# Signs of 64-bit weights as one byte written by GpSimd, two VectorE operations in place of three, each weight tile begun one tile ahead

## The chip, the cores and the metric

One core of a Trainium2 chip runs the kernel. The metric is the device time of one execution in microseconds (us); lower is better. PE is TensorE (its weight loads are PEld), DVE is VectorE, ACT is ScalarE, POOL is GpSimd, SP is SyncE, whose queue issues the transfers.

## The reference

Attention over 8 batches with 8 heads of width 64, on 512 local and 32 global positions, and then a feed-forward layer over the resulting 8 x 544 = 4352 tokens (the kernel works them as eight blocks of 512 local rows and a last one of the 256 global rows):

```python
k_all, v_all = concat(k_g, k_l), concat(v_g, v_l)
out_g = softmax(scale * q_g @ k_all.T) @ v_all              # 32 global rows see all
s_ll = where(|i - j| <= 32, scale * q_l @ k_l.T, -1e9)      # 512 local rows: a band ...
a_l = softmax(concat(scale * q_l @ k_g.T, s_ll))            # ... and the 32 global keys
x = concat(out_g, a_l @ v_all), heads side by side          # tokens x 512
h = x @ w_in                                                # 512 x 2048
g = max(h, 0) + log1p(exp(-abs(h)))
return g @ w_out                                            # 2048 x 512
```

The attention's inputs are 32-bit floats. The two weight matrices arrive as 64-bit floats. The kernel loads them as pairs of 32-bit words and makes 32-bit floats of them on the chip.

## The kernel before

**Stages.** Heads are worked in pairs; m numbers the 32 pairs, four to a batch. The first four pairs (batch 0's, m = 0 to 3, in two parts each) go through a stage written out by hand: scores, `soft0` (the maximum L169, its scaling L170, the exps L172 on ACT, the sums' L178 and L179), diagonal matrices on POOL (L185), `turn0`, `evict0` (L213), `values0` and `split0` (L231). The global rows of that stage use L254 and L255. Every later m goes in pieces with two parts, (m, 0) and (m, 1): scores into the PSUM tiles `s_ps`, copied to SBUF by ACT (L310) or DVE (L312); the maxima by a transposing reduction (L313) and a gather of small operations (POOL L325, DVE L328 to L338); `probs` spreads them as a mask `mb` (two DVE transposes, L346), POOL subtracts it (L355, L357) and ACT takes the exps (L358); the sums by a second transposing reduction (L368) with its own gather (L325 to L332, L371, L375), spread as `rb` (L377); the values into the PSUM tile `v_ps`, scaled by DVE into `xa` (L396). `s_ps` and `v_ps` use banks in turn, so PE can't write the next scores or values into a bank before L310, L312 or L396 has read it. The attention's result is split into a high and a low part, `xh` (L442) and `xl` (L443), whose matmuls together keep the precision.

**Feed-forward.** Its work comes in items between the pieces of attention: an item multiplies `xh` and `xl` by a tile of w_in into `h`; ACT and DVE make softplus of it (L530 to L532 on ACT, `e` by DVE L533), which is split into `gh` (ACT L536) and `gl` (POOL L537), and these are multiplied by tiles of w_out into `o`. The number in `e_5` counts these steps.

**Weights.** There are 32 tiles, 16 of each matrix (`wi`, `wo`), of 128 x 512 pairs of words. One is loaded as `wiraw` or `woraw` and goes through `split_w`:

- `abs_w`: ACT (L470) scales the high word, read as a 32-bit float, by a power of two into `wbits`. That puts its exponent right for the shift that follows.
- `bits_w`: DVE shifts `wbits` left by 3 (L477), puts the sign of the high word in (L479), and puts in the three top bits of the low word (L482). The result stands in the low words' places, or for the last tile of a matrix in `wlast`.
- `halves_w`: ACT rounds it to the matmul's format (L487), and POOL subtracts that from it (L488), which gives the low half.

`wbits` of some tiles, `wlast` and the masks `mb` take turns in two buffers called "mb".

**What sets the order.** PE's order is the order in which the program is written. The other engines' order comes from a scheduler at build time, which follows dependences and priorities, with some pins: `keep` and, in the hand-written stage (while `tight` is true), `note` chain operations of an engine one behind the other; `after(i, "maxima")` holds a weight operation behind the latest maxima on DVE. In the hand-written stage one weight tile is worked per step, for W_PRE = 9 steps; later `weights(upto)` works tiles up to a mark that runs ahead of the items.

Of the kernel before, what the change touches and what calls it, by code (L numbers as in the profile page):

```python
# [19 lines left out]
P = 128  # L20
# [10 lines left out]
NF = DFF // P  # L31
# [32 lines left out]
def moe_over_global_local_attention(  # L64
# [34 lines left out]
    for o, w, base, sign in ((32, 32, 0, 1), (64, 32, -96, -1), (96, 128, 32, 1), (96, 128, 32, -1)):  # L99
        r = mask0[:, 0, 1, o:o + w]  # L100
# [55 lines left out]
    def keep(what, i):  # L156
        order[what] = after(i, what).ins
# [184 lines left out]
    def probs(m, p):  # L342
        s, e = st["s", m, p], st["e", m]
        k = QW[p] // 32
        mb = pl.tile([P, 2, 352], F32, tag="mb", name=f"mb{m}_{p}", bufs=2)
        nc.vector.transpose(mb[:, :, :QW[p]].rearrange("p h (s k) -> p h s k", k=32),  # L346
                            windows(e, FIRST[p], 21, 2, k).unsqueeze(3).to_broadcast([P, 2, k, 32]))

        def pairs(t, width, start, step, w):
            base = t[:, 0, start:start + 1]  # L350
            return bass.AP(base.tensor, base.offset, [list(base.ap[0]), [width, 2], [step, 2], [1, w]])

        for so, sd, mo, md, w in (((0, 352, 0, 192, 160),), ((32, 192, 0, 128, 192),))[p]:
            sw = pairs(s, 512, so, sd, w)
            nc.gpsimd.tensor_tensor(sw, sw, pairs(mb, 352, mo, md, w), op=ALU.subtract)  # L355
        for so, mo, w in (((160, 64, 192),), ((0, 64, 32), (416, 224, 96)))[p]:
            nc.gpsimd.tensor_tensor(s[:, :, so:so + w], s[:, :, so:so + w], mb[:, :, mo:mo + w], op=ALU.subtract)  # L357
        nc.scalar.activation(s, s, AF.Exp, scale=0.125)  # L358
# [87 lines left out]
    wi, wo, raws = {}, {}, {}  # L446
# [13 lines left out]
    def note(what, i):  # L460
        if tight:
            keep(what, i)
        return i

    def abs_w(kind, k):
        if A_LO <= k < NF - A_UP:
            a = pl.tile([P, 512], I32, tag=f"{kind}{k + A_UP}", name=f"wbits{kind}{k}", bufs=1)
        else:
            a = pl.tile([P, 512], I32, tag="mb", name=f"wbits{kind}{k}", bufs=2)
        note("act", nc.scalar.mul(a.bitcast(F32), raws[kind, k][:, :, 1].bitcast(F32), DOWN))  # L470
        return a

    def bits_w(kind, k, a):
        t = raws.pop((kind, k))
        lo32, hi32 = t[:, :, 0], t[:, :, 1]

        i = nc.vector.tensor_scalar(a, a, 3, None, op0=ALU.logical_shift_left)  # L477
        note("dve", i) if tight else after(i, "maxima")
        note("dve", nc.vector.scalar_tensor_tensor(a, hi32, -0x80000000, a, op0=ALU.bitwise_and, op1=ALU.bitwise_or))  # L479

        r = lo32 if k < NF - 1 else pl.tile([P, 512], I32, tag="mb", name=f"wlast{kind}", bufs=2)
        note("dve", nc.vector.scalar_tensor_tensor(r, lo32, 29, a, op0=ALU.logical_shift_right, op1=ALU.bitwise_or))  # L482
        return r.bitcast(F32)

    def halves_w(kind, k, r):
        (wi if kind == "wi" else wo)[k] = o = pl.tile([P, 2, 512], F32R, tag=f"{kind}{k}", name=f"{kind}{k}", bufs=1)
        note("act", nc.scalar.copy(o[:, 0], r))  # L487
        nc.gpsimd.tensor_tensor(o[:, 1], r, o[:, 0].bitcast(F32), op=ALU.subtract)  # L488

    def split_w(kind, k):  # L490
        halves_w(kind, k, bits_w(kind, k, abs_w(kind, k)))

    def output_banks():
        if "o" not in banks:
# [147 lines left out]
    tight, held = True, None  # L642
    for k in range(-2, n - 2):
        stage(k + 2, 0)
        if k == 0:
            key_masks()
        if held:
            r = bits_w(*held)
        stage(k + 2, 1)
        stage(k - 2, 5)  # L650
        stage(k - 2, 6)
        stage(k, 3)
        stage(k, 4)
# [16 lines left out]
    tight = False  # L670
# [74 lines left out]
```

## Time and profile before

| | |
|---|---|
| median of 3 runs | 990.09 us (990.07 to 990.39) |
| the profiled execution's own time | 991.48 us |
| its span in the trace | 989.7 us |
| mean granted TensorE clock | 0.988 |
| busy: PE, PEld | 946.2 us (96%), 763.8 us (77%) |
| busy: DVE, ACT, POOL | 643.1 us (65%), 492.6 us (50%), 469.5 us (47%) |
| the 32 weight tiles on DVE: L477, L479, L482 | 21.5 us, 28.7 us, 29.8 us |
| the 32 weight tiles on POOL: L488 | 45.2 us |

In a row of the timeline stand the start and the duration in us, engine, line, operation, output and inputs; behind it in brackets the idle time of that engine just before and what ended it. In a row that groups operations stand their count, their busy time in us and the mean of one in ns, and behind the second bar the idle time before them. In a row by stretch stand the stretch, its length, the busy time of each engine, the granted clock, the share of the DMA engines and their GB/s. The release of a wait is inferred from the semaphores.

### The profile page before, as it was taken

To read this page: it belongs to the slowest core of one execution; us is meant where nothing else is said; L and a number is where in the kernel's file an instruction comes from. 1 tells how busy PE (TensorE), PEld (TensorE's weight loads), DVE (VectorE), ACT (ScalarE), POOL (GpSimd) and SP (SyncE) were. 2 spreads that over 40 slices of the span, in tenths; PEclk is the share of its full clock that TensorE was granted. 3 is DMA by queue.
4 is the path that set the end of the run, shared out by engine and by line. 5 is a ranking of instruction groups with operands and counts; after the bars stand their busy time and mean duration, and the time that the engine had idled before them with its cause. 6 is when DMAs were issued, how large, how long until landed. Compare 5 with 4: busy or idle time off the path is not lost.

```text
span 989.7 us, 14732 instructions
## 1 busy us (share of the span) xinstructions
PE 946.2 (96%) x5476; PEld 763.8 (77%) x5476; DVE 643.1 (65%) x1193; ACT 492.6 (50%) x811; POOL 469.5 (47%) x648
## 2 busy tenths in 40 slices
PE   6998598889999999999999999999999999999998
PEld 4776476668888788878887888878887888888896
DVE  5869898896667756786669666776668665411211
ACT  5756466544444544454445444454454445444453
POOL 4437776655445544444445544554445444322221
PEclk8998899999999999999999999999999999999999
DMA  9651331211112211121112111121112100100000
GB/s 357 231 188 46 122 111 57 65 66 41 47 47 69 69 47 46 48 74 47 47 37 72 47 47 47 66 71 47 47 33 88 32 17 1 65 1 1 10 35 22
DMA packets 30697, 64.60 MB, mean 65 GB/s; under 512 B 7328, under 2 KB 7840, under 8 KB 30624
## 3 DMA queue, kind: packets, MB, share of 16 engines
q1 hardware_dynamic: 29888, 63.32, 19.0%
q8 instruction: 43, 0.70, 0.3%
q10 hardware_dynamic: 736, 0.33, 0.2%
q14 instruction: 30, 0.25, 0.1%
HBM read 54.20 MB, written 9.44 MB: 64 GB/s over the span
## 4 chain that ended last, share of the span: by engine, by line
PE 67%; DVE 9%; POOL 4%; issue 3%; ACT 1%; DMA 1%; POOLq 0%; DVEq 0%; ACTq 0%
PE o L132 30%; PE h L132 29%; PE s_ps L132 5%; PE v_ps L132 4%; DVE xh L442 1%; DVE zt L368 1%; DVE xl L443 1%; POOL xl L443 1%; DVE mb L346 1%; POOL mt L325 1%; DVE s L312 1%; POOL s L355 1%; DVE xa L396 1%; DVE mt L332 0%; DVE e L533 0%
## 5 line engine op out<-in xcount | busy, mean ns | idle before, releaser
L132 PE MATMUL h<-xh,wi 128*128 128x512 f32 (+1 forms) x1152 | 341.9, 380 | 6.5 <-DVE e L533 5.8
L132 PE MATMUL o<-wo,gh 128*128 128x512 f32 x1088 | 344.8, 398 | 0.0
L537 POOL TENSOR_TENSOR gl<-e,gh 128x512 fp32r<-128x512 f32 x136 | 180.5, 1327 | 315.7 <-ACT gh L536 263.2
L132 PEld LDWEIGHTS h<-xh,wi 128*128 128x128 f32 x1152 | 211.1, 188 | 51.8 <-DVE e L533 8.9
L132 PEld LDWEIGHTS o<-wo,gh 128*128 128x128 f32 x1088 | 198.8, 188 | 46.0 <-issue 3.3
L533 DVE SCALAR_TENSOR_TENSOR e<-h,e 128x512 f32<-128x512 f32 x136 | 92.7, 682 | 210.1 <-ACT e L532 192.5
L132 PE MATMUL h<-xl,wi 128*128 128x512 f32 (+1 forms) x576 | 217.6, 378 | 0.9 <-DVE xl L443 0.9
L132 PE MATMUL o<-wo,gl 128*128 128x512 f32 x544 | 213.1, 392 | 0.2
L530 ACT ACTIVATE e<-h 128x512 f32<-128x512 f32 x136 | 81.0, 595 | 175.5 <-PE h L132 173.5
L536 ACT CAST gh<-e 128x512 fp32r<-128x512 f32 x136 | 84.5, 622 | 154.7 <-DVE e L533 154.5
L132 PEld LDWEIGHTS h<-xl,wi 128*128 128x128 f32 x576 | 108.4, 188 | 21.7 <-DVE xl L443 1.3
L355 POOL TENSOR_TENSOR s<-s,mb 128x640 f32<-128x640 f32 (+1 forms) x56 | 96.6, 1725 | 57.8 <-DVE mb L346 57.8
L132 PEld LDWEIGHTS o<-wo,gl 128*128 128x128 f32 x544 | 102.4, 188 | 23.2 <-POOL gl L537 1.1
L368 DVE TRANSPOSE_TENSOR_REDUCE zt<-s 128x32 f32<-128x1024 f32 x56 | 69.4, 1239 | 58.9 <-ACT s L358 58.7
L358 ACT ACTIVATE s<-s 128x1024 f32<-128x1024 f32 x56 | 59.4, 1061 | 83.5 <-POOL s L357 47.7
L532 ACT ACTIVATE e<-e,one 128x512 f32<-128x512 f32 x136 | 98.4, 723 | 4.3
L531 ACT ACTIVATE e<-e 128x512 f32<-128x512 f32 x136 | 85.9, 632 | 3.9
L313 DVE TRANSPOSE_TENSOR_REDUCE mt<-s 128x32 f32<-128x1024 f32 x56 | 68.9, 1231 | 3.7 <-ACT s L310 2.9
L132 PE MATMUL s_ps<-raw 64*128 64x192 f32 (+2 forms) x672 | 64.3, 325 | 0.6 <-issue 0.6
L132 PEld LDWEIGHTS v_ps<-s,v 128*64 128x64 f32 x896 | 49.4, 137 | 19.5 <-ACT s L310 6.5
L132 PE MATMUL v_ps<-s,v 128*64 128x96 f32 (+3 forms) x896 | 56.7, 280 | 7.3 <-ACT s L310 5.2
L132 PEld LDWEIGHTS s_ps<-raw 64*128 64x128 f32 x672 | 53.5, 192 | 11.6 <-issue 10.8
(147 smaller groups left out, 886.0 us busy)
## 6 DMA issues: line engine op xcount, KB each, us to landing
raw<-in_qk SPq DMA_DIRECT2D x32, 352.0 KB, 3.0
v<-in_v SPq DMA_DIRECT2D x28, 384.0 KB, 3.0
raw<-in_qk SPq DMA_DIRECT2D x28, 368.0 KB, 3.6
wiraw<-in_w_in SPq DMA_DIRECT2D x16, 512.0 KB, 8.5
woraw<-in_w_out SPq DMA_DIRECT2D x16, 512.0 KB, 7.4
out<-ot SPq DMA_DIRECT2D x32, 256.0 KB, 2.1
v<-in_v SPq DMA_DIRECT2D x4, 512.0 KB, 8.6
raw<-in_qk SPq DMA_DIRECT2D x4, 416.0 KB, 8.3
```

Source lines behind the costliest of these rows:

```text
L132: order["pe"] = after(nc.tensor.matmul(*a, **k), "pe").ins
L313: order["scores"] = nc.vector.tensor_reduce(windows(mt, 4 + 16 * p, 36, 2, 16), s.rearrange("p h (b k) -> p h b k", k=32), axis=AX.X, op=A ...
L355: nc.gpsimd.tensor_tensor(sw, sw, pairs(mb, 352, mo, md, w), op=ALU.subtract)
L358: nc.scalar.activation(s, s, AF.Exp, scale=0.125)
L368: nc.vector.tensor_reduce(windows(zt, 4 + 16 * p, 36, 2, 16), st["s", m, p].rearrange("p h (b k) -> p h b k", k=32), axis=AX.X, op=ALU.add ...
L443: (nc.vector if j % 2 else nc.gpsimd).tensor_tensor(lo, f(t), hi.bitcast(F32), op=ALU.subtract)
L530: nc.scalar.activation(e, ph, AF.Abs)
L531: nc.scalar.activation(e, e, AF.Exp, scale=-1.0)
L532: nc.scalar.activation(e, e, AF.Ln, bias=one)
L533: nc.vector.scalar_tensor_tensor(e, ph, 0.0, e, op0=ALU.max, op1=ALU.add)
L536: nc.scalar.copy(gh, e)
L537: nc.gpsimd.tensor_tensor(gl, e, gh.bitcast(F32), op=ALU.subtract)
```

## The change

DVE's three operations on a tile become two, and POOL gets a small one:

- `signs_w` (new): DVE shifts the low word right by 29 in place (new L475), which leaves its three top bits at the bottom and zeros above. POOL (new L477) compares the high word, read as a float, with 0, multiplies by 128, and writes the result as one byte, the top byte of that shifted low word.
- `bits_w`: one DVE operation (new L483) shifts `wbits` left by 3 and puts in the low word with its sign byte.
- `begin_w` (new): a tile's `signs_w` and `abs_w`; `weights` calls it for a tile and for the one behind it ahead of `split_w`. The pin behind the maxima is now on L475, no longer on the shift of `wbits`.
- In the hand-written stage `begin_w` is called where `abs_w` was, at the end of the step before; L475 is chained there, so it stands ahead of the next L169.
- The buffers "mb" are three, no longer two.

The later lines move by the inserted ones: L487 and L488 become L488 and L489, L530 to L533 become L541 to L544, L536 and L537 become L547 and L548.

```diff
-        mb = pl.tile([P, 2, 352], F32, tag="mb", name=f"mb{m}_{p}", bufs=2)
+        mb = pl.tile([P, 2, 352], F32, tag="mb", name=f"mb{m}_{p}", bufs=3)
...
+    def signs_w(kind, k):
+        t = raws[kind, k]
+        note("dve", i := nc.vector.tensor_scalar(t[:, :, 0], t[:, :, 0], 29, None, op0=ALU.logical_shift_right))
+        b = t.rearrange("p c w -> p (c w)").bitcast(mybir.dt.uint8).rearrange("p (c b) -> p c b", b=8)
+        nc.gpsimd.tensor_scalar(b[:, :, 3], t[:, :, 1].bitcast(F32), 0.0, 128.0, op0=ALU.is_lt, op1=ALU.mult)
+        return i
+
     def bits_w(kind, k, a):
         t = raws.pop((kind, k))
-        lo32, hi32 = t[:, :, 0], t[:, :, 1]
-
-        i = nc.vector.tensor_scalar(a, a, 3, None, op0=ALU.logical_shift_left)
-        note("dve", i) if tight else after(i, "maxima")
-        note("dve", nc.vector.scalar_tensor_tensor(a, hi32, -0x80000000, a, op0=ALU.bitwise_and, op1=ALU.bitwise_or))
-
-        r = lo32 if k < NF - 1 else pl.tile([P, 512], I32, tag="mb", name=f"wlast{kind}", bufs=2)
-        note("dve", nc.vector.scalar_tensor_tensor(r, lo32, 29, a, op0=ALU.logical_shift_right, op1=ALU.bitwise_or))
+        r = t[:, :, 0] if k < NF - 1 else pl.tile([P, 512], I32, tag="mb", name=f"wlast{kind}", bufs=3)
+        note("dve", nc.vector.scalar_tensor_tensor(r, a, 3, t[:, :, 0], op0=ALU.logical_shift_left, op1=ALU.bitwise_or))
         return r.bitcast(F32)
...
+    begun = {}
+
+    def begin_w(kind, k):
+        if (kind, k) not in begun:
+            i = signs_w(kind, k)
+            if not tight:
+                after(i, "maxima")
+            begun[kind, k] = abs_w(kind, k)
+        return kind, k, begun[kind, k]
+
     def split_w(kind, k):
-        halves_w(kind, k, bits_w(kind, k, abs_w(kind, k)))
+        halves_w(kind, k, bits_w(*begin_w(kind, k)))
...
             if order_w[wk[1]]:
+                begin_w(*order_w[wk[1]])
+                if wk[1] + 1 < len(order_w) and order_w[wk[1] + 1]:
+                    begin_w(*order_w[wk[1] + 1])
                 split_w(*order_w[wk[1]])
...
         if -1 <= k and wk[1] < W_PRE:
-            held = order_w[wk[1]]
-            held += (abs_w(*held),)
+            held = begin_w(*order_w[wk[1]])
```

PE's order is the same before and after. DVE's order at three places follows. In a row stand the line, the operation, the output and its input, and the shape; a number at the end of a name only tells tiles apart, and the one or two before it say which part (`xa_0` is m = 4's, `xa_1` m = 5's; `e_5` the fifth step).

First, DVE in the hand-written stage, one step near 43 us; before:

```order
L213 COPY p_1_0gl<-t_1_0_348 96x512
L169 TENSOR_REDUCE sums_1_376<-s_2_1_368 128x4
L170 TENSOR_SCALAR sums_1_376<-sums_1_376 128x4
L477 TENSOR_SCALAR wbitswi_366<-wbitswi_366 128x512
L479 SCALAR_TENSOR_TENSOR wbitswi_366<-wiraw_127,wbitswi_366 128x512
L482 SCALAR_TENSOR_TENSOR wiraw_127<-wiraw_127,wbitswi_366 128x512
L178 TENSOR_SCALAR sums_1_376<-sums_1_376 128x4
```

and after:

```order
L213 COPY p_1_0gl<-t_1_0_348 96x512
L475 TENSOR_SCALAR wiraw_127<-wiraw_127 128x512
L169 TENSOR_REDUCE sums_1_378<-s_2_1_370 128x4
L170 TENSOR_SCALAR sums_1_378<-sums_1_378 128x4
L483 SCALAR_TENSOR_TENSOR wiraw_127<-wbitswi_368,wiraw_127 128x512
L178 TENSOR_SCALAR sums_1_378<-sums_1_378 128x4
```

The three operations between L170 and L178 became one, and the new shift stands between L213 and L169.

Second, DVE around L396 of m = 4, which frees the PSUM bank for which PE stands at 120.37 us; before (from e_4 on):

```order
L313 TENSOR_REDUCE mt_906<-s_1_1048 128x2x16
...
L338 COPY mt_906<-mt_906 32x40 x3
L477 TENSOR_SCALAR wbitswo_1121<-wbitswo_1121 128x512
L477 TENSOR_SCALAR wbitswo_1175<-wbitswo_1175 128x512
L477 TENSOR_SCALAR wbitswo_1290<-wbitswo_1290 128x512
L346 STREAM_TRANSPOSE mb_0_1064<-mt_906 128x704
L346 STREAM_TRANSPOSE mb_1_1069<-mt_906 128x2x320
L479 SCALAR_TENSOR_TENSOR wbitswo_1121<-woraw_953,wbitswo_1121 128x512
L533 SCALAR_TENSOR_TENSOR e_5_1110<-h_5_1087,e_5_1110 128x512
L396 TENSOR_TENSOR xa_0_1146<-v_ps_1129,rb_981 128x384
```

and after:

```order
L313 TENSOR_REDUCE mt_910<-s_1_1052 128x2x16
L483 SCALAR_TENSOR_TENSOR wiraw_932<-wbitswi_1035,wiraw_932 128x512
L328 TENSOR_REDUCE zt_967<-zt_967 32x6x2 x2
...
L375 RECIPROCAL zr_980<-zt_967 32x19 x4
L377 STREAM_TRANSPOSE rb_985<-zr_980 128x608
L396 TENSOR_TENSOR xa_0_1150<-v_ps_1133,rb_985 128x384
L396 TENSOR_TENSOR xa_0_1150<-v_ps_1133,rb_985 128x224
L544 SCALAR_TENSOR_TENSOR e_5_1114<-h_5_1091,e_5_1114 128x512
L328 TENSOR_REDUCE mt_910<-mt_910 32x6x2 x2
```

L396 stood behind the gather and the transposes of the next maxima; now it stands ahead of them, behind its own sums' gather, and ahead of e_5.

Third, DVE ahead of L396 of m = 5, for which PE stands at 148.77 us; before:

```order
L533 SCALAR_TENSOR_TENSOR e_8_1371<-h_8_1348,e_8_1371 128x512
L332 COPY mt_1192<-mt_1192 32x6
L338 COPY mt_1192<-mt_1192 32x40 x3
L346 STREAM_TRANSPOSE mb_0_1337<-mt_1192 128x704
L346 STREAM_TRANSPOSE mb_1_1342<-mt_1192 128x2x320
L396 TENSOR_TENSOR xa_1_1419<-v_ps_1402,rb_1248 128x384
```

and after:

```order
L368 TENSOR_REDUCE zt_1234<-s_0_912 128x2x16
L368 TENSOR_REDUCE zt_1234<-s_1_1052 128x2x16
...
L544 SCALAR_TENSOR_TENSOR e_8_1375<-h_8_1352,e_8_1375 128x512
...
L346 STREAM_TRANSPOSE mb_0_1341<-mt_1196 128x704
L346 STREAM_TRANSPOSE mb_1_1346<-mt_1196 128x2x320
L475 TENSOR_SCALAR wiraw_1218<-wiraw_1218 128x512
...
L375 RECIPROCAL zr_1247<-zt_1234 32x19 x4
L544 SCALAR_TENSOR_TENSOR e_9_1452<-h_9_1431,e_9_1452 128x512
L377 STREAM_TRANSPOSE rb_1252<-zr_1247 128x608
L396 TENSOR_TENSOR xa_1_1423<-v_ps_1406,rb_1252 128x384
```

The transposing reductions L368 of m = 5 were long done at that place before (they stood ahead of e_6 and e_7); now they, with e_9, stand between e_7 and L396. On ACT, L358 of m = 5, which L368 reads, stood ahead of `s_1` of m = 6's copy (L310), and now follows it.

More of the change, by code (lines that the diff above doesn't have):

```diff
@@ L468, in abs_w @@
         else:
-            a = pl.tile([P, 512], I32, tag="mb", name=f"wbits{kind}{k}", bufs=2)
+            a = pl.tile([P, 512], I32, tag="mb", name=f"wbits{kind}{k}", bufs=3)
         note("act", nc.scalar.mul(a.bitcast(F32), raws[kind, k][:, :, 1].bitcast(F32), DOWN))
         return a
+    def signs_w(kind, k):
[4 more added lines that the diff above has]
+        return i
     def bits_w(kind, k, a):
         t = raws.pop((kind, k))
-        lo32, hi32 = t[:, :, 0], t[:, :, 1]
-        i = nc.vector.tensor_scalar(a, a, 3, None, op0=ALU.logical_shift_left)
-        note("dve", i) if tight else after(i, "maxima")
-        note("dve", nc.vector.scalar_tensor_tensor(a, hi32, -0x80000000, a, op0=ALU.bitwise_and, op1=ALU.bitwise_or))
-        r = lo32 if k < NF - 1 else pl.tile([P, 512], I32, tag="mb", name=f"wlast{kind}", bufs=2)
-        note("dve", nc.vector.scalar_tensor_tensor(r, lo32, 29, a, op0=ALU.logical_shift_right, op1=ALU.bitwise_or))
+        r = t[:, :, 0] if k < NF - 1 else pl.tile([P, 512], I32, tag="mb", name=f"wlast{kind}", bufs=3)
+        note("dve", nc.vector.scalar_tensor_tensor(r, a, 3, t[:, :, 0], op0=ALU.logical_shift_left, op1=ALU.bitwise_or))
         return r.bitcast(F32)
```

## The prediction

> **What bounds the kernel now.** I read the page's head first, then TensorE's waits, then stretches of the span, then the operations that are exchanged.
>
> The page:
>
> ```profile
> span 989.7 us, 14732 instructions
> ...
> PE 946.2 (96%) x5476; PEld 763.8 (77%) x5476; DVE 643.1 (65%) x1193; ACT 492.6 (50%) x811; POOL 469.5 (47%) x648
> ```
>
> PE is idle for 989.7 - 946.2 = 43.5 us in all; no other engine bounds the whole. Busy time by stretch (PE, PEld, DVE, ACT, POOL, then the granted clock):
>
> ```profile
> 75.00:100.00 25.00, 22.59 (x109) 17.55 (x110) 24.93 (x40) 16.15 (x28) 17.59 (x16) 0.86 0.16 50
> 100.00:125.00 25.00, 14.88 (x86) 10.88 (x86) 21.75 (x31) 12.32 (x20) 17.86 (x18) 0.86 0.29 107
> 225.00:300.00 75.00, 75.00 (x437) 60.67 (x437) 48.25 (x97) 34.88 (x51) 36.41 (x57) 1.00 0.12 37
> ```
>
> From 225 us on PE has no gap, and all weight tiles are done by then: the change can act only ahead of that. In 75 to 100 DVE is full (24.93 of 25), and in 100 to 125 PE loses ten of 25 us. So the question is which PE waits before 225 end on DVE. PE's waits of more than 1 us behind the first 20 us, as its timeline has them (start, duration, then the idle time ahead and what ended it):
>
> ```profile
> 47.13 1.13 PE L132 MATMUL s0g<-raw,raw 128*128 128x256 f32 x4 [1.67 <-ACT e L172]
> 77.41 1.10 PE L132 MATMUL o0g<-p0g1gh,v 128*128 128x64 f32 x8 [2.72 <-ACT p0g1gh L254]
> 102.09 0.73 PE L132 MATMUL h<-xh,wi 128*128 128x512 f32 x2 [1.19 <-DVE e L533]
> 106.50 1.70 PE L132 MATMUL v_ps<-s,v 128*64 128x160 f32 x26 [1.40 <-ACT s L310]
> 120.37 1.03 PE L132 MATMUL s_ps<-mask,ident 128*128 128x512 bf16 x2 [7.54 <-DVE xa L396]
> 148.77 0.60 PE L132 MATMUL s_ps<-mask,ident 128*128 128x512 bf16 x2 [1.24 <-DVE xa L396]
> 169.60 1.70 PE L132 MATMUL v_ps<-s,v 128*64 128x160 f32 x26 [3.36 <-ACT s L310]
> 197.13 2.03 PE L132 MATMUL v_ps<-s,v 128*64 128x160 f32 x32 [2.05 <-DVE s L312]
> 216.16 0.73 PE L132 MATMUL h<-xh,wi 128*128 128x512 f32 x2 [1.66 <-DVE e L533]
> ```
>
> The reader is to see that none of these waits names a weight operation: they end on DVE and ACT work that stands in a row with the weight operations. What counts is not the time saved on DVE but what now stands ahead of xa (L396), L310, L172 and e (L533).
>
> **What is exchanged.**
>
> ```profile
> L479 DVE SCALAR_TENSOR_TENSOR wbitswo<-woraw,wbitswo 128x512 int32<-128x512 int32 x16 | 14.7, 921 | 0.2
> ...
> L479 DVE SCALAR_TENSOR_TENSOR wbitswi<-wiraw,wbitswi 128x512 int32<-128x512 int32 x16 | 14.0, 873 | 0.2
> ...
> L477 DVE TENSOR_SCALAR wbitswo<-wbitswo 128x512 int32<-128x512 int32 x16 | 11.5, 727 | 0.2 <-ACT wbitswo L470 0.2
> L477 DVE TENSOR_SCALAR wbitswi<-wbitswi 128x512 int32<-128x512 int32 x16 | 10.0, 624 | 0.0
> ...
> L488 POOL TENSOR_TENSOR wi<-wiraw,wi 128x512 fp32r<-128x512 f32 x15 | 20.7, 1377 | 4.0 <-ACT wi L487 4.0
> L101 POOL TENSOR_SCALAR_AFFINE_SELECT mask<-mask 128x128 bf16<-128x128 bf16 x2 | 0.6, 294 | 0.0
> L101 POOL TENSOR_SCALAR_AFFINE_SELECT mask<-mask 128x32 bf16<-128x32 bf16 x2 | 0.4, 214 | 0.0
> ```
>
> - *Off DVE*: L479, 28.7 us over 32 tiles.
> - *L477 becomes new L475* (a shift of every other word) and L482 becomes new L483 (the same two-input operation). New L475 lies between 0.41 (L477 unhindered, the row at 45.07 below) and 0.69 (the two-input form unhindered, at 45.52); nearest is L477, the same operation, so 0.42. New L483 has the form of L479 and L482: 0.69.
> - *On POOL*: new L477 there, a one-input operation on 512 columns that writes bytes. No row shows one. Lower bound: the selects at 32 and 128 columns give (294 - 214) / 96 = 0.83 ns a column, 0.214 + 480 x 0.00083 = 0.61 us. Upper bound: L488 with its two inputs, 1.3 (the row at 97.07 shows one hindered, 1.76; mean 1.377). Between ends this far apart I take 1.0, since byte writes at a stride are farther from the bf16 select than from L488's strided input; both ends go into the range. It adds 32 us to POOL in the first 225 us. New L483 waits for it, and it waits in POOL's row behind the subtractions; behind that L483 on DVE stand the e operations (L533, for whose gh and gl PE waits) and the gathers. Beginning a tile ahead is to cover this; where POOL is a whole tile late, the cover is gone, and POOL's next operation of 1.3 is what is late (rival B).
> - *ACT* keeps L470 and the cast. No DMA is added. The third buffer of "mb" is space alone: at most it lets a weight tile or a mask wait less.
>
> In all DVE loses nearly 29 us of work, against some 20 us of PE waits that it could shorten. The new order decides.
>
> **The terms**, on the time axis of the profile before.
>
> *1, the first 47 us.* DVE runs a loop with ACT (L213, L169, L170, exps L172, L178):
>
> ```profile
> 43.67 1.08 DVE L169 TENSOR_REDUCE sums<-s 128x4 f32<-128x896 f32 x1
> ...
> 45.07 0.41 DVE L477 TENSOR_SCALAR wbitswi<-wbitswi 128x512 int32<-128x512 int32 x1
> 45.52 0.69 DVE L479 SCALAR_TENSOR_TENSOR wbitswi<-wiraw,wbitswi 128x512 int32<-128x512 int32 x1
> ...
> 47.11 0.17 DVE L178 TENSOR_SCALAR sums<-sums 128x4 f32<-128x4 f32 x1 [0.17 <-ACT e L172]
> ```
>
> The three weight operations lay under the exps, for which L178 then still waits 0.17: taking them away gains nothing. The new L475 stands ahead of L169, in the loop itself, in seven rounds up to 47 us: 7 x 0.42 = 2.9, and PE is already 1.67 late there, so it passes on. +3.0 (2 to 4). A longer idle stretch can also lower the clock afterwards (term 4): +1 (0 to 3).
>
> *2, 70 to 78 us.* After the maxima of m=4 DVE now runs four L475, the two transposes, five L475, then e_1, which the chain to PE's 2.72 wait at 77.41 needs (L254 stands behind gh_1 on ACT). Before: L477, transposes, L479, L482, e_1. Unhindered, 9 x 0.42 = 3.8 replaces 0.41 + 0.69 + 0.69 = 1.8; by the means above the three took 0.62 + 0.87 + 0.87 = 2.4, hindered by POOL. Of the 1.4 to 2.0 more I take +1, since the slack of POOL and ACT behind e_1 is not seen (-1 to +4).
>
> *3, 102 and 106 us.* DVE arrives with about ten tiles' L479 less: of 1.19 + 1.40, -2.2.
>
> *4, 120 us.* xa of m=4 stood behind the maxima of m=5, three L477, two transposes and an L479; now it comes ahead of e_5. Of the 7.54 wait 0 to 2 remain. After it the clock was low:
>
> ```profile
> 120.00:130.00 10.00, 9.63 (x42) 7.37 (x43) 10.00 (x12) 7.66 (x12) 9.15 (x9) 0.81 0.29 107
> ```
>
> 0.19 x 10 = 1.9 us of clock goes too if the wait does. -8.5 (-9.4 to -6.5).
>
> *5, 149 us.* xa of m=5 now has ahead of it, behind ACT's L358 of m=5: two L368, three L483, e_8, both gathers, two transposes of m=6, four L475, L375 x4, e_9 and L377. And L358 has moved behind L310 of m=6 (first ACT's row for that L310, then DVE's prices):
>
> ```profile
> 140.13 1.01 ACT L310 COPY s<-s_ps 128x1024 f32<-128x1024 f32 x1
> ...
> 128.80 1.20 DVE L368 TRANSPOSE_TENSOR_REDUCE zt<-s 128x32 f32<-128x1024 f32 x1
> ...
> 137.75 1.10 DVE L375 RECIPROCAL zr<-zt 32x19 f32<-32x19 f32 x4
> 138.88 0.69 DVE L533 SCALAR_TENSOR_TENSOR e<-h,e 128x512 f32<-128x512 f32 x1
> ...
> 140.80 0.80 DVE L377 STREAM_TRANSPOSE rb<-zr 128x608 f32<-128x608 f32 x1
> ...
> 144.18 0.55 DVE L328 TENSOR_REDUCE mt<-mt 32x12 f32<-32x96 f32 x2 [1.46 <-POOL mt L325]
> ...
> 146.33 1.64 DVE L346 STREAM_TRANSPOSE mb<-mt 128x704 f32<-128x704 f32 x2
> 147.90 0.81 DVE L396 TENSOR_TENSOR xa<-v_ps,rb 128x384 f32<-128x384 f32 x2
> ```
>
> L310 ends at 141.1; then come a scaling and a cast of some 0.65 each (as L470 at 166.55 below) and the first L358 of about 1.1: 143.5. DVE then needs two L368 (2.4), two L483 (1.4; a third fits into a wait), the maxima's gather with e_8 in it (144.18 to 146.33: 2.15), the sums' gather (about 1.5, the same without L338), the transposes (1.64), four L475 (1.7), L375 (1.1), e_9 (0.69) and L377 (0.8): 13.4, less some 1.5 by which starts overlap ends: 155.4, and 156.2 with xa, against 148.7 before. PE, whose order is fixed, waits here: +7.5, and +0.3 of low clock: +7.8 (0 to 10).
>
> *6, 170 us.* Before, L310 of m=7 stood behind a scaling that waited for a transfer:
>
> ```profile
> 166.55 0.66 ACT L470 ACTIVATE wbitswi<-wiraw 128x512 f32<-128x512 f32 x1 [0.57 <-DMA wiraw<-in_w_in]
> ...
> 168.54 1.01 ACT L310 COPY s<-s_ps 128x1024 f32<-128x1024 f32 x1
> ```
>
> It now stands ahead of it: -3.3 of 3.36.
>
> *7, 185 us.* The last w_in tile's L483 now comes behind e_13, its cast and L488 end near 186.3, and h_14 wants the tile's second half at 184.55, with no wait now:
>
> ```profile
> 184.55 0.62 PE L132 MATMUL h<-xh,wi 128*128 128x512 f32 x2
> ```
>
> +1.7 (0 to 3).
>
> *8, 197 to 216 us.* L312 comes earlier (of 2.05, -2), the last xa and a gl later (+2.2, from the same drift as in 5): +0.2 (-3 to +3).
>
> Sum: 3.0 + 1.0 + 1.0 - 2.2 - 8.5 + 7.8 - 3.3 + 1.7 + 0.2 = +0.7. The profiled execution took 991.48 (989.7 of span and 1.8 around it), 1.39 above the median of 990.09: 992.2 for it, 990.8 for the median.
>
> **The port.** Rows first: a POOL subtraction and DVE's weight operations stretch each other.
>
> ```profile
> 97.07 1.76 POOL L488 TENSOR_TENSOR wo<-woraw,wo 128x512 fp32r<-128x512 f32 x1
> ...
> 97.58 1.53 DVE L477 TENSOR_SCALAR wbitswo<-wbitswo 128x512 int32<-128x512 int32 x1
> ...
> 88.40 3.26 POOL L537 TENSOR_TENSOR gl<-e,gh 128x512 fp32r<-128x512 f32 x1 [2.96 <-ACT gh L536]
> ```
>
> L477 takes 1.53 for 0.41, gl 3.26 for 1.33. If the two never overlap, a tile takes 0.41 + 0.69 + 0.69 + 1.30 = 3.1 before and 0.42 + 0.69 + 1.0 + 1.30 = 3.4 after: what DVE gives up comes back as waiting. The Trainium skill, SBUF — State Buffer, section "Who interferes with whom", calls the pair of ports that DVE and GpSimd share an exclusive lock, which the loser awaits for a whole instruction; the rows agree. By that rule alone the change would lose 0.3 x 32 = 10 us of joint engine time, and the sum would come out as in rival B. Another page speaks for the change: GPSIMD Engine Reference, section 4.1 "Engine selection", has one-input operations at roughly line rate, so the sign would cost near the lower end; the sum would then be about 1 us lower. No run here shows it.
>
> **Rivals.**
> - *A, faster.* The new order costs nothing at 149: term 5 is 0 and the rest stands, 990.8 - 7.8 = 983.0. For it: DVE is far less loaded by then, and e_8, e_9 may come early. Against it: L358's place behind L310. It decides if L358 ends before 138. 0.30.
> - *B, slower.* The sign takes 1.3, and at 70 to 78 us L475 after L475 waits for a POOL operation as at 97.58: up to eight times 0.9 = 7, which delays e_1 and the 77.41 wait by as much: 990.8 + 7 = 998, more with the low clock behind it. It decides once nine L475 together take over 6 us. 0.20.
> - *C, no relief at 120*: xa of m=4 waits for its sums as long as before; +8.5 on the sum, 999. Against it: the sums come before the maxima in the new order. 0.05.
>
> **Chances.** The forecast 0.45, with its own range 986 to 996 (0.08 of it faster, 0.20 within, 0.17 slower); A 0.30 (0.28 faster, 0.02 within); B 0.20 and C 0.05, all slower. A change under 0.2% (2.0 us) can't be told from none: faster 0.36, same 0.22, slower 0.42. The range: from A with the sign at 0.61, 982, to B with its bounds, 1001.
>
> **What would show it.** Right: the 7.54 wait gone, a wait on xa of 5 us or more near 149, the early loop's L169 some 3 us later by 47 us, the 3.36 gone, DVE's weight work down by about 28 us. Wrong: POOL's sign outside 0.6 to 1.3; L475 means above 1; no wait near 149; a new wait for a weight tile (h or o on L488) in the first 225 us.

## The result: 30 us slower, outside the range

| | median | runs | ratio to before |
|---|---|---|---|
| before | 990.08 us | 4, 989.85 to 990.39 | |
| changed | 1020.73 us | 4, 1019.94 to 1024.81 | 1.0318 (1.029 to 1.0345) |

The forecast was 990.8 us with a range of 982 to 1001. The profiled execution of the changed kernel is the one of 1024.81 us, 4 us above the median, so its places lie somewhat late. One of the five executions of run e6 below, 1057.93 us at a granted clock of 0.845 where the other four had 0.986 to 0.989, is in a slow state and left out of its figures.

The head of the page of the changed kernel:

```profile
span 1023.0 us, 14699 instructions
...
PE 959.4 (94%) x5469; PEld 774.5 (76%) x5476; DVE 625.5 (61%) x1161; ACT 494.8 (48%) x811; POOL 544.4 (53%) x680
```

DVE lost 17.6 us of busy time (643.1 to 625.5), POOL gained 74.9 (469.5 to 544.4). The span grew by 33.3 us (989.7 to 1023.0): PE's idle time by 20.1 (43.5 to 63.6), and its busy time by 13.2 (946.2 to 959.4) for the same matmuls, at a mean granted clock of 0.970 where it was 0.988. So some two fifths of the longer span are the same work at a lower clock. The groups of the operations that were exchanged (count, busy us, mean ns, then the idle time ahead):

```profile
L477 POOL TENSOR_SCALAR wiraw<-wiraw 128x512 uint8<-128x512 f32 x16 | 43.2, 2744 | 0.0
L477 POOL TENSOR_SCALAR woraw<-woraw 128x512 uint8<-128x512 f32 x16 | 43.0, 2719 | 1.7 <-DVE woraw L475 1.7
...
L475 DVE TENSOR_SCALAR woraw<-woraw 128x512 int32<-128x512 int32 x16 | 15.9, 1014 | 1.7 <-DMA woraw<-in_w_out 1.7
L483 DVE SCALAR_TENSOR_TENSOR woraw<-wbitswo,woraw 128x512 int32<-128x512 int32 x15 | 15.5, 1046 | 9.8 <-POOL woraw L477 9.5 <-ACT wbitswo L470 0.2
...
L483 DVE SCALAR_TENSOR_TENSOR wiraw<-wbitswi,wiraw 128x512 int32<-128x512 int32 x15 | 13.7, 913 | 19.5 <-POOL wiraw L477 18.7 <-ACT wbitswi L470 0.8
L475 DVE TENSOR_SCALAR wiraw<-wiraw 128x512 int32<-128x512 int32 x16 | 12.4, 788 | 0.9 <-DMA wiraw<-in_w_in 0.9
```

The sign takes 2.73 us on POOL, where the forecast took 1.0 and bounded it at 1.3. DVE stands idle for 28.2 us ahead of L483 until the sign is done. The hand-written stage in the timeline, POOL's rows of one step and a half first, then DVE's:

```profile
25.43 1.16 POOL L185 TENSOR_TENSOR diag(1, 1)_308<-identf,sums 128x512 f32<-128x512 f32 x1 [1.10 <-DVE sums L179]
26.55 1.48 POOL L489 TENSOR_TENSOR wi<-wiraw,wi 128x512 fp32r<-128x512 f32 x1
28.00 2.69 POOL L477 TENSOR_SCALAR wiraw<-wiraw 128x512 uint8<-128x512 f32 x1
31.85 1.04 POOL L185 TENSOR_TENSOR diag(2, 0)_361<-identf,sums 128x512 f32<-128x512 f32 x1 [1.17 <-DVE sums L179]
...
26.79 1.08 DVE L169 TENSOR_REDUCE sums<-s 128x4 f32<-128x896 f32 x1
27.90 0.17 DVE L170 TENSOR_SCALAR sums<-sums 128x4 f32<-128x4 f32 x1
30.72 0.69 DVE L483 SCALAR_TENSOR_TENSOR wiraw<-wbitswi,wiraw 128x512 int32<-128x512 int32 x1 [2.64 <-POOL wiraw L477]
31.33 0.16 DVE L178 TENSOR_SCALAR sums<-sums 128x4 f32<-128x4 f32 x1
```

The reader is to see a ring: the diagonal (about 1.0), the subtraction (1.5), the sign (2.7), then L483 and the inverse sums on DVE (1.2), and the next diagonal. It takes 6.4 us here (25.43 to 31.85) and 6.3 in the mean of six steps; before, the mean of the same six was 5.0 (4.6 in places, as from L169 at 39.07 to the next at 43.67). POOL is never idle in it except for DVE, and ACT's exps no longer set the step. Later in the span, POOL's row ahead of a gl, and PE's wait for it:

```profile
152.49 2.67 POOL L477 TENSOR_SCALAR woraw<-woraw 128x512 uint8<-128x512 f32 x1
154.97 1.31 POOL L489 TENSOR_TENSOR wo<-woraw,wo 128x512 fp32r<-128x512 f32 x1
156.22 1.73 POOL L548 TENSOR_TENSOR gl<-e,gh 128x512 fp32r<-128x512 f32 x1
...
158.01 0.80 PE L132 MATMUL o<-wo,gl 128*128 128x512 f32 x1 [9.10 <-POOL gl L548]
...
181.61 0.61 PE L132 MATMUL s_ps<-mask,ident 128*128 128x512 bf16 x1 [12.11 <-DVE xa L396]
```

Before, no PE wait ended on gl. Now two do, 14.5 us together.

### The profile page after: what moved, and what is told of

Same layout as the page of the kernel before. It is cut to its first block, busy times and chain, and to the rows that moved or that the text cites. A ratio compares the mean times of both kernels' runs of the same rounds, so it can differ in the third digit from the quotient of the medians.

```text
span 1023.0 us, 14699 instructions
## 1 busy us (share of the span) xinstructions
PE 959.4 (94%) x5469; PEld 774.5 (76%) x5476; DVE 625.5 (61%) x1161; ACT 494.8 (48%) x811; POOL 544.4 (53%) x680
## 4 chain that ended last, share of the span: by engine, by line
PE 72%; DVE 11%; POOL 11%; issue 4%; ACT 1%; DMA 0%; ACTq 0%; POOLq 0%; SPq 0%; DVEq 0%
PE o L132 31%; PE h L132 30%; PE s_ps L132 6%; PE v_ps L132 4%; POOL wiraw L477 3%; POOL woraw L477 2%; POOL wi L489 1%; DVE xh L442 1%; DVE zt L368 1%; DVE xl L443 1%; DVE mb L346 1%; POOL gl L548 1%; POOL wo L489 1%; POOL mt L325 1%; DVE mt L338 1%
## 5 line engine op out<-in xcount | busy, mean ns | idle before, releaser
L132 PE MATMUL o<-wo,gh 128*128 128x512 f32 x1088 | 348.7, 402 | 0.0
L548 POOL TENSOR_TENSOR gl<-e,gh 128x512 fp32r<-128x512 f32 x136 | 176.2, 1296 | 310.7 <-ACT gh L547 258.5
L132 PEld LDWEIGHTS o<-wo,gh 128*128 128x128 f32 x1088 | 201.2, 191 | 47.0 <-issue 3.4
L544 DVE SCALAR_TENSOR_TENSOR e<-h,e 128x512 f32<-128x512 f32 x136 | 92.8, 683 | 223.1 <-ACT e L543 207.6
L132 PE MATMUL o<-wo,gl 128*128 128x512 f32 x544 | 215.5, 396 | 14.5 <-POOL gl L548 14.5
L541 ACT ACTIVATE e<-h 128x512 f32<-128x512 f32 x136 | 80.8, 594 | 199.0 <-PE h L132 191.9
L547 ACT CAST gh<-e 128x512 fp32r<-128x512 f32 x136 | 84.4, 620 | 148.0 <-DVE e L544 147.4
L368 DVE TRANSPOSE_TENSOR_REDUCE zt<-s 128x32 f32<-128x1024 f32 x56 | 69.4, 1240 | 64.3 <-ACT s L358 64.3
L358 ACT ACTIVATE s<-s 128x1024 f32<-128x1024 f32 x56 | 59.4, 1060 | 78.3 <-POOL s L357 43.1
L132 PE MATMUL s_ps<-raw 64*128 64x192 f32 (+2 forms) x672 | 63.6, 322 | 2.9 <-issue 2.8
L132 PEld LDWEIGHTS s_ps<-raw 64*128 64x128 f32 x672 | 52.9, 190 | 13.2 <-issue 13.2
L312 DVE TENSOR_TENSOR s<-s_ps,mask 128x1024 f32<-128x1024 f32 x48 | 58.2, 1212 | 5.3 <-PE s_ps L132 5.2
```

The lines of the kernel that those rows point to most:

```text
L132: order["pe"] = after(nc.tensor.matmul(*a, **k), "pe").ins
L312: nc.vector.tensor_tensor(s, ps, mask[:, p].unsqueeze(1).to_broadcast([P, 2, 512]), op=ALU.add)
L368: nc.vector.tensor_reduce(windows(zt, 4 + 16 * p, 36, 2, 16), st["s", m, p].rearrange("p h (b k) -> p h b k", k=32), axis=AX.X, op=ALU.add ...
L541: nc.scalar.activation(e, ph, AF.Abs)
L544: nc.vector.scalar_tensor_tensor(e, ph, 0.0, e, op0=ALU.max, op1=ALU.add)
L547: nc.scalar.copy(gh, e)
```

## The experiments

Two theories stand: P, the price of the sign on GpSimd and those who wait for it; and O, the new order, which would cost even if the sign were free.

**The price list.** A kernel of its own runs GpSimd's forms one behind the other on 128x512:

```diff
+        p.tensor_scalar(bytes_of(s, 512), hi, 0.0, 128.0, op0=ALU.is_lt, op1=ALU.mult)     # L88, the sign
...
+        p.tensor_scalar(bytes_of(s, 512), hi, 0.0, None, op0=ALU.is_lt)                     # L90
+        p.tensor_scalar(bytes_of(s, 512), hi, 2.0, 128.0, op0=ALU.mult, op1=ALU.add)        # L91
+        p.tensor_scalar(bytes_of(s, 512), x, 0.0, 128.0, op0=ALU.is_lt, op1=ALU.mult)      # L92
...
+        p.tensor_scalar(u, x, 0.0, 128.0, op0=ALU.is_lt, op1=ALU.mult)                      # L94, u: bytes in a row
+        p.tensor_scalar(f, x, 0.0, 128.0, op0=ALU.is_lt, op1=ALU.mult)                      # L95
+        p.tensor_scalar(f, x, 0.0, None, op0=ALU.is_lt)                                     # L96
+        p.tensor_scalar(f, x, 2.0, None, op0=ALU.mult)                                      # L97
+        p.tensor_scalar(f, x, 2.0, 128.0, op0=ALU.mult, op1=ALU.add)                        # L98
...
+        p.tensor_tensor(f, hi, x, op=ALU.subtract)                                          # L101
+        p.tensor_scalar(s[:, :, 0].bitcast(F32), hi, 0.0, 128.0, op0=ALU.is_lt, op1=ALU.mult)   # L102
...
```

> This kernel computes nothing of the reference. It runs GpSimd's one-input operation on 128x512 in eleven forms, one behind the other (one or two arithmetic steps, a comparison or not, input every other word or contiguous, output as bytes every eighth, as contiguous bytes, or as floats), and a copy and two-input operations for scale; then the sign operation on VectorE and the scaling on ScalarE. What is to be told apart is why the sign took 2.7 us in the changed kernel and not 0.6 to 1.3. Theory S (two arithmetic steps): the form with one step takes 1.4 or less, floats or bytes. Theory B (bytes at a stride): the same two steps to contiguous floats take 1.3 or less. Theory K (the comparison): multiply and add take 1.3 or less. Theory G (any TENSOR_SCALAR on GpSimd at this size): all eleven forms take 2 us or more, and 256 columns take about half.

Its groups (s are bytes at every eighth place, in L102 floats at every other place; u are bytes in a row, f floats in a row; words are every other word, x in a row):

```profile
L88 POOL TENSOR_SCALAR s<-words 128x512 uint8<-128x512 f32 x2 | 6.4, 3208 | 2.6 <-DMA words<-in_w_in 2.6
L92 POOL TENSOR_SCALAR s<-x 128x512 uint8<-128x512 f32 x2 | 5.3, 2632 | 0.0
L90 POOL TENSOR_SCALAR s<-words 128x512 uint8<-128x512 f32 x2 | 4.4, 2212 | 0.0
...
L102 POOL TENSOR_SCALAR s<-words 128x512 f32<-128x512 f32 x2 | 3.9, 1965 | 0.0
L95 POOL TENSOR_SCALAR f<-x 128x512 f32<-128x512 f32 x2 | 3.8, 1917 | 0.0
L94 POOL TENSOR_SCALAR u<-x 128x512 uint8<-128x512 f32 x2 | 3.8, 1916 | 0.0
L97 POOL TENSOR_SCALAR f<-x 128x512 f32<-128x512 f32 x2 | 3.0, 1488 | 0.0
L96 POOL TENSOR_SCALAR f<-x 128x512 f32<-128x512 f32 x2 | 3.0, 1484 | 0.0
...
L91 POOL TENSOR_SCALAR s<-words 128x512 uint8<-128x512 f32 x2 | 2.6, 1318 | 0.0
...
L101 POOL TENSOR_TENSOR f<-words,x 128x512 f32<-128x512 f32 x2 | 2.6, 1290 | 0.0
...
L98 POOL TENSOR_SCALAR f<-x 128x512 f32<-128x512 f32 x2 | 1.2, 622 | 0.0
```

S (one step, 1.4 or less), B (floats in a row, 1.3 or less) and G (2 us or more in all) fall. K holds to the letter, as multiply and add takes 0.62 to floats in a row, but its reason doesn't: a comparison alone takes 1.48 and a multiplication alone 1.49. Compare and multiply takes 1.92, multiply and add 0.62, as the copy does (0.63). So the pair of steps sets the price, and multiply and add is the cheap pair. To bytes at every eighth place the same forms take 0.7 more (L92 against L95, L91 against L98). Bytes in a row add nothing (L94), and floats at every other place, which have the same distance of eight bytes, add next to nothing (L102 with 1.97, its strided input included). It is bytes and stride together that cost, neither the stride nor the type alone. 1.92 and 0.7 make 2.6, and the sign in the kernel took 2.64 at the least and 2.73 in the mean. (The first L88 ran beside VectorE's work and took 3.37; the second, 3.05, did so only for its first half us, and the rest of its excess is not explained.) The lower bound of the forecast, 0.61, happens to be the price of another pair of steps; the upper, 1.30, is the price of a two-input form (L101), and even a single step of the one-input form is above it.

**Without the sign, and with the sign on VectorE.**

```diff
-        nc.gpsimd.tensor_scalar(b[:, :, 3], t[:, :, 1].bitcast(F32), 0.0, 128.0, op0=ALU.is_lt, op1=ALU.mult)
```

> The changed kernel without GpSimd's sign operation: the sign is left out, so all weights are positive. All else is as in the changed kernel: two VectorE operations, begun one tile ahead, three buffers. Theory P (price): the sign's 2.7 us on GpSimd and those who wait for it are the whole of the 30 us, and the rest of the forecast's sum holds; then this takes 983 to 992 us, the early loop's period falls from 6.28 back to 4.6 to 5.0 us, and the waits on gl at 110 and 158 us are gone. Theory O (order): the new order on VectorE (shifts of many tiles ahead of the masks' transposes, xa of m=5 behind the sums) costs most of it by itself; then this takes 1005 us or more, and PE still waits about 12 us on xa of m=5.

982.04 us (ratio 0.9912, 0.9897 to 0.9926): 1 us below theory P's range, and 8.5 us faster than before. The early step fell to 5.0 us, no PE wait on gl was left, and PE waited 5.3 us on xa of m=4 but only 0.2 on xa of m=5. So the order had changed with the operation: without it the scheduler places some 70 rows of DVE elsewhere. This run alone can't part the price from the order.

```diff
-        nc.gpsimd.tensor_scalar(b[:, :, 3], ...
+        note("dve", nc.vector.tensor_scalar(b[:, :, 3], ...
```

> The changed kernel with the sign byte written by VectorE in the same form, so VectorE has three operations for a tile again, but begun a tile ahead. Theory P: GpSimd is free of it, so 985 to 997 us, as VectorE's work is about that of the kernel before and the early loop gets one more operation ahead of L169 (8 x 0.4 to 0.7 us). Theory O: 1005 us or more. If VectorE too takes 2 us for the byte form, 1010 or more.

1010.23 us (1.0197, 1.0182 to 1.0212): a miss for P's 985 to 997, and a time that O's 1005 or more allows. On DVE the form took 1.16 and 1.36 us in the mean, where I had reckoned with 0.4 to 0.7, and it stands with L475 ahead of L169: the early step took 6.5 us in the mean of six. This points to the reason of the forecast's first term (what stands ahead of L169 is paid in each step), but the order moved here too, so it doesn't decide against O.

**The order held still.** In the next five runs each instruction of DVE, ACT, POOL and SP is pinned behind the one that stands ahead of it in the changed kernel, so all five have its order row for row. The sign comes from ScalarE, whose scaling becomes a leaky rectifier with a slope of 2^32 for negative numbers: that sets the bit which the shift by 3 moves into the sign's place. GpSimd's operation stays in its row, with another price; f1's writes zeros.

```diff
-        note("act", nc.scalar.mul(a.bitcast(F32), raws[kind, k][:, :, 1].bitcast(F32), DOWN))
+        note("act", nc.scalar.activation(a.bitcast(F32), raws[kind, k][:, :, 1].bitcast(F32), AF.Prelu, scale=DOWN, alpha=2.0 ** 32))
...
-        nc.gpsimd.tensor_scalar(b[:, :, 3], t[:, :, 1].bitcast(F32), 0.0, 128.0, op0=ALU.is_lt, op1=ALU.mult)
+        nc.gpsimd.tensor_scalar(b[:, :, 3], t[:, :, 1].bitcast(F32), 0.0, 0.0, op0=ALU.mult, op1=ALU.add)             # f1
+        nc.gpsimd.tensor_scalar(b[:, :n, 3], t[:, :n, 1].bitcast(F32), 0.0, 128.0, op0=ALU.is_lt, op1=ALU.mult)       # f2: n = 16
+        n = 512 if tight else 16                                                                                       # f3; f4 the reverse
+        nc.gpsimd.tensor_scalar(scratch.bitcast(mybir.dt.uint8)...[:, :, len(begun) % 4], t[:, :, 1].bitcast(F32), ...)            # f5, the rest as before
```

> The changed kernel with every engine held to the changed kernel's order, row for row; GpSimd's operation writes the same bytes but multiplies and adds (it writes zeros), which took 1.32 us in the price list, near the 1.0 of the forecast; the sign itself comes from ScalarE's leaky rectifier. Theory P (the price was the one step that failed): 990 to 996 us, which is the forecast's 990.8 with 0.3 us more for a sign; PE still waits 5 to 9 us on xa of m=5. Theory O (the order costs it): 1005 or more. Theory T (a threshold: GpSimd's sign costs nothing until it is slower than the loop around it): 983 to 988.

> The same frozen order, with GpSimd's sign operation on 16 of 512 columns (about 0.15 us): the order without the price. Theory P: 984 to 990, and what is left of PE's wait on xa of m=5 is the order's own cost (5 to 8 us by the forecast's fifth term). Theory O: 1005 or more. If the forecast's fifth term is wrong: no wait on xa of m=5 above 2 us, and 978 to 984.

> The same frozen order, with the full sign operation in the nine tiles of the hand-written stage alone and 16 columns in the 23 later ones. In the changed kernel a step of that stage took 6.28 us where it took 4.6 before; its GpSimd row (sign 2.66, a wait of 1.1, diagonal 1.04, subtraction 1.48) closes a ring with VectorE. Theory P, split by place: about 8 x 1.65 = 13 us above the run with the tiny sign everywhere, less 2 us of slack that PE had.

> The same frozen order, with 16 columns in the nine early tiles and the full sign operation in the 23 later ones. Theory P, split by place: the rest of the difference between the changed kernel (1020.7) and the tiny sign, some 20 us above the run with the tiny sign, with the waits on gl behind two signs (5.4 and 9.1 us) and the larger wait on xa of m=5. If early and late do not add up to the whole within 3 us, the two places share slack.

> The changed kernel in its own order on every engine, with the full comparison on GpSimd for all 32 tiles, but its bytes go to a scratch tile (every fourth byte), so no VectorE operation waits for it and it waits for none; the sign comes from ScalarE's leaky rectifier. Theory Q (GpSimd's row is occupied: diagonals, gl and subtractions stand behind the signs): 1010 to 1020 us, near the changed kernel. Theory W (VectorE's L483 waits for the sign, and what stands behind it): 1000 us or less, near the tiny sign's 992.3.

| run | a sign on POOL, mean us | median us | ratio to before |
|---|---|---|---|
| f2, tiny | 0.40 | 992.26 | 1.0019 (1.0008 to 1.0031) |
| f3, full in the 9 early tiles | 2.67 there | 1002.08 | 1.0109 (1.0094 to 1.0124) |
| f4, full in the 23 later tiles | 2.76 there | 1011.83 | 1.0213 (1.0198 to 1.0228) |
| f1, cheap | 1.43 | 1007.26 | 1.0159 (1.014 to 1.0178) |
| f5, full, awaited by none | 2.27 | 1005.16 | 1.0154 (1.0132 to 1.0176) |
| the changed kernel | 2.73 | 1020.73 | 1.0318 (1.029 to 1.0345) |

(f5 writes every fourth byte, which is cheaper than every eighth.) What follows:

- *Not the order.* With the tiny sign the new order costs 992.26 - 990.45 = 1.8 us over the runs of before at its side, a little above P's 984 to 990 and far from O's 1005. O falls. If the 15 us for each us of price (next point) held down to nothing, the tiny sign itself would carry some 6 of these us (an estimate), and the order alone would save time; no run shows that.
- *The price.* From 0.40 to 1.43 us a sign costs 15.0 us, from 1.43 to 2.73 another 13.5: 15 and 10 us for each us of price. Theory T (a sign costs nothing until it is slower than the loop around it) falls, as a sign of 1.43 us already costs; where between 0.40 and 1.43 the cost begins, no run shows. f1 was a miss for P as I had put it (990 to 996) and lies where O was expected; f2, with the same order, is what decides between them. A sign of 1.4 us is far from hidden. Part of these us is the clock: for the same matmuls PE is busy for 945.8 us in f2, 953.2 in f1 and 959.4 in the changed kernel.
- *The places add up.* Early 9.8 and late 19.6 make 29.4; the whole is 28.5 (the changed kernel, whose order is not pinned and whose sign is GpSimd's own). Early, the expected 13 less 2 came to 9.8; the 13 was reckoned from steps of 4.6 us, and their mean before was 5.0. Late, PE's waits on gl are back in f4 with 14.6 us, where f2 has none.
- *Occupation and waiting, about half each.* f5's row is occupied by 72 us of signs, and nobody reads their result: 12.9 us over the tiny sign. That is neither Q's 1010 to 1020 nor W's 1000 or less. On the line from f1 to the changed kernel an awaited sign of 2.27 would come to some 1016 (an estimate), 23.7 over the tiny one. So both Q and W hold a part, and the halves rest on that estimate. DVE's rows are longer beside the full signs, 625.3 us in f5 and 625.5 in the changed kernel for 617.1 in f2; these 8 us are inside both parts. The row of POOL in f5 still makes PE wait for gl:

```profile
PE o L133 <- POOL gl L550: 12.6, 3, 8.9
PE s_ps L133 <- DVE xa L397: 12.2, 1, 12.2
```

**Two operations on VectorE, none on GpSimd.** The leaky rectifier makes the sign's byte superfluous. Four runs try it without held order. The first is the kernel before with this alone:

```diff
-        i = nc.vector.tensor_scalar(a, a, 3, None, op0=ALU.logical_shift_left)
+        i = nc.vector.tensor_scalar(t[:, :, 0], t[:, :, 0], 29, None, op0=ALU.logical_shift_right)
...
-        note("dve", nc.vector.scalar_tensor_tensor(a, hi32, -0x80000000, a, op0=ALU.bitwise_and, op1=ALU.bitwise_or))
...
-        note("dve", nc.vector.scalar_tensor_tensor(r, lo32, 29, a, op0=ALU.logical_shift_right, op1=ALU.bitwise_or))
+        note("dve", nc.vector.scalar_tensor_tensor(r, a, 3, t[:, :, 0], op0=ALU.logical_shift_left, op1=ALU.bitwise_or))
```

> The kernel before, with its order of calls and two buffers, but ScalarE's scaling is a leaky rectifier with slope 2^32 for negative numbers, which puts the sign where the shift by 3 takes it, so VectorE needs two operations and GpSimd none. Theory P: the relief of VectorE that the change was to give, without GpSimd's price: 970 to 988 us. Theory O in its strong form (VectorE's load ahead of 225 us is not what PE waits for): 988 to 992.

984.08 us (0.9932, 0.9915 to 0.9949): the relief of DVE is worth 6.5 us, inside P's range. The other three add parts of the change: e4 all of it but GpSimd's operation (begun ahead everywhere, three buffers), e5 begins ahead in the later tiles alone, e6 has the three buffers alone (`bufs=2` to `bufs=3`).

```diff
     def bits_w(kind, k, a):
+        if tight:                          # e5: the early tiles' shift under the exps
+            signs_w(kind, k)
...
         if (kind, k) not in begun:
-            i = signs_w(kind, k)
             if not tight:
-                after(i, "maxima")
+                after(signs_w(kind, k), "maxima")
```

> The changed kernel without GpSimd's operation (so the program of the run without a sign), with the sign from ScalarE's leaky rectifier: nothing is left out. If the scaling with a slope costs what the plain scaling does (0.665 against 0.659 us in the price list): 980 to 984 us, as that run's 982.0.

> The same, but in the hand-written stage the shift stands behind L170, under the exps, as the weight operations did before; only the later tiles are begun ahead. If the forecast's first term holds (an operation in the early loop costs its duration): 1 to 3 us below the run begun ahead everywhere, 978 to 982. If PE's slack hides it: the same within 1 us.

> The kernel before with the leaky rectifier and two VectorE operations (984.1 with two buffers), now with three buffers for the masks and weight bits, nothing begun ahead. If the buffer is what the begun-ahead form gains by: 981 to 983. If it is space alone: 983.5 to 984.7.

e4 took 983.23 us (0.9926, 0.9913 to 0.9938), e5 980.72 (0.9902, 0.9889 to 0.9916) and e6 983.90 (0.9933, 0.9919 to 0.9947), each inside a range expected for it. The buffers are space alone, as e6 takes what e3 takes. e5 is 2.5 us under e4 and the fastest kernel here, 9.5 us under the kernel before. What the 2.5 us are made of is not settled, and the runs of the two touch (e4 981.39 to 984.23, e5 980.49 to 981.74). In the profiles PE's first scores of the global rows start at 47.38 us in e4 and at 45.04 in e5, but so does the clock differ: the stretch from 20 to 25 us, e4 first, then e5 (the granted clock stands third from the end):

```profile
20.00:25.00 5.00, 5.00 (x23) 3.78 (x22) 2.58 (x7) 3.54 (x11) 2.51 (x3) 0.52 1.03 402
...
20.00:25.00 5.00, 4.61 (x46) 3.74 (x45) 3.89 (x9) 3.47 (x12) 2.37 (x3) 1.00 1.03 403
```

A clock of 0.52 for 5 us is 2.4 us of TensorE, about as much as the whole difference. It came behind a PE wait of 3.65 us at 19 us in e4; in e5 that wait was 1.93. Whether the shift in the loop or the clock made it, these runs don't part.

## Why the prediction was wrong, step by step

f2 has the changed kernel's order with a sign of almost no price, so its waits show the order's terms by themselves (start, idle time ahead):

```profile
47.38 1.13 PE L133 MATMUL s0g<-raw,raw 128*128 128x256 f32 x4 [1.76 <-ACT e L173]
...
80.12 1.97 PE L133 MATMUL o0g<-p0g1gh,v 128*128 128x64 f32 x8 [5.39 <-ACT p0g1gh L255]
...
152.27 0.61 PE L133 MATMUL s_ps<-mask,ident 128*128 128x512 bf16 x1 [13.59 <-DVE xa L397]
187.38 0.51 PE L133 MATMUL h<-xh,wi 128*128 128x512 f32 x1 [0.68 <-ACT wi L490]
189.36 0.50 PE L133 MATMUL h<-xh,wi 128*128 128x512 f32 x1 [1.47 <-POOL wi L491]
```

The clock behind the long wait in f2 (0.77 for 13 us, 3.0 us of TensorE), and the early stretches of the kernel before, where PE is busy without a gap at a clock of 0.52 and then 1.00:

```profile
152.00:165.00 13.00, 12.38 (x50) 9.78 (x52) 6.38 (x8) 6.89 (x11) 3.33 (x7) 0.77 0.00 1
...
20.00:25.00 5.00, 5.00 (x24) 3.60 (x24) 2.86 (x7) 3.54 (x11) 2.42 (x3) 0.52 1.03 402
25.00:30.00 5.00, 5.00 (x56) 4.17 (x57) 4.59 (x10) 3.56 (x12) 1.17 (x2) 1.00 1.04 396
30.00:45.00 15.00, 15.00 (x142) 12.68 (x138) 13.78 (x29) 10.49 (x31) 7.26 (x7) 1.00 0.63 241
```

| term | forecast | f2 against before |
|---|---|---|
| 1, early loop | +3.0 and +1.0 of clock | +0.25 (s0g at 47.38 for 47.13; the clock is low in both) |
| 2, 70 to 78 us | +1.0 | +2.5 (o0g at 80.12 for 77.41, less 0.25) |
| 3, 102 and 106 us | -2.2 | -2.6 (both waits gone) |
| 4, xa of m=4 | -8.5 | -7.5 (the wait is gone) and -1.9 of clock |
| 5, xa of m=5 | +7.8 | +12.35 (13.59 for 1.24) and +3.0 of clock |
| 6, L310 of m=7 | -3.3 | -3.4 (gone) |
| 7, last tile of w_in | +1.7 | +2.15 (0.68 and 1.47) |
| 8, 197 to 216 us | +0.2 | -2.8 (2.05 gone, 0.90 for 1.66) |
| sum | +0.7 | +2.0 by these, +1.8 by the medians |

That the sum meets the medians is luck. The two profiled executions it is read from differ by -0.3 us (spans of 989.4 and 989.7), and the waits below 1 us that f2 lost beside those of the table (0.86, 0.61, 0.45 and 0.21) make 2.1, which brings +2.0 to -0.1.

- **The failed step is the sign's price and what it holds up.** "Between ends this far apart I take 1.0" and "Upper bound: L488 with its two inputs, 1.3" fell: 2.73. I took it for granted that an operation with one input costs no more than one with two. From the price list, 0.7 of it is that bytes are written at a stride and 1.3 is the pair of compare and multiply over multiply and add. The Trainium skill's GPSIMD Engine Reference, section 4.1 "Engine selection", has one-input operations at roughly line rate; in the price list the copy takes 0.63 and multiply and add the same, so the rule can fit these two at most: this pair takes three times that.
- **"Beginning a tile ahead is to cover this" fell too.** The sum held no term for POOL's row at all. Even at 1.0 a sign would have cost about 9 us by the line from f2 to f1 (0.6 x 14.6), an estimate, as no run has a sign of that price; so the forecast of 990.8 would have been some 1001. By the same estimate the miss of 30 us is 1.5 of the order, 9 of cover that wasn't there, and 20 of price.
- **Why a tile ahead doesn't cover.** In the hand-written stage the sign of a tile is issued one step ahead of its use, but behind that step's diagonal and subtraction; the slack is only the rest of the step, and POOL's row (5.2 of busy time in a step) closes the ring through L483. Later, two or three signs in a row (7.7 us at 180 us) stand ahead of a gl.
- **The ordering terms held in sign, the eighth aside.** The waits of 7.54 and 3.36 us are gone in the changed kernel, and PE waits 12.1 us on xa of m=5, as named. Term 5 was too small: PE, no longer held up at 120, comes to that place at 138.7, ten us before xa was ready in the kernel before, and its low clock afterwards was put at 0.3 for 3.0. Term 1 was too large. I had read PE's wait of 1.67 us at 47 as a sign that DVE sets the early stage; the stretches above show that PE has no gap from 20 to 45 us there. Its clock was low at 20 to 25, which is the likely reason: in e5, with 1.00 in that stretch, PE has gaps of 2.4 us up to 45. Under the low clock f2's step on DVE, longer by L475, was hidden. In the changed kernel the ring through POOL was too long to hide.
- **Rival B** named the place (nine L475 took 7.0 us in the changed kernel, its mark was 6), the direction and GpSimd, but took its price from the same bound of 1.3; PE's wait there grew by only 1.2 us (2.72 to 3.89), and by more with the tiny sign (5.39 in f2). **Rival A** needed term 5 to be 0, and it was 12. **Rival C** didn't come.
- Of the signs named ahead, "POOL's sign outside 0.6 to 1.3" is the one that showed it, and L475's mean was above 1 for the tiles of w_out (1.014) alone. The "new wait for a weight tile" came with 0.94 and 1.22 us, about as the seventh term has it; the large new wait, 14.5 us on gl, no sign had named. DVE's weight operations went from 80.0 to 59.1 us with the last tiles, 21 less and not the 28 named, since L475 and L483 are stretched beside POOL's work.

## What to carry to other kernels

A price bounded by rows of other operations is no bound: where a change rests on a form that the trace doesn't show, give its price an open upper end, or time it in a small list of forms first. An operation that moves to an idle-looking engine is paid in that engine's row: ask what stands behind it there, and whether its result closes a ring with those who feed that engine, before its share of busy time is believed. To part an operation's price from the order that a scheduler makes of it, hold the order and vary the price; and look for a free place in an operation that runs anyway, as the scaling on ScalarE had for the sign.

## What the runs showed of the hardware

- GpSimd on 128x512 floats in a row: multiply and add 0.62 us, copy 0.63, multiply alone 1.49, compare alone 1.48, compare and multiply 1.92. A subtraction of two inputs, one of them every other word, took 1.29. An added step can make the one-input operation faster, and one input can cost more than two.
- Writing bytes at every eighth place adds 0.7 us to compare and multiply (2.63), to compare alone (2.21), and to multiply and add (1.32); bytes in a row (1.92) add nothing, and floats at the same distance (1.97) next to nothing.
- The leaky rectifier on ScalarE took 0.665 us beside 0.659 for the plain scaling: a different slope for negative numbers cost 0.006 us there.
- The granted clock from 20 to 25 us was 0.52 behind a TensorE wait of 3.65 us (e4) and of 3.31 (before), 0.75 behind one of 3.31 (e3) and 1.00 behind one of 1.93 (e5): the wait's length alone doesn't give it.
